# Attention decode with an MLP: output weights loaded later, a part of them by 32 one-row GpSimd transfers that alternate with 2-byte ones

## The chip, the cores and the metric

The kernel runs on one core of one Trainium2 chip. The metric is the time of the core for one execution in microseconds (us), measured on the device. Every figure of a kernel below is the median of its runs unless it says otherwise.

In the profile, PE is the tensor engine, DVE the vector engine, ACT the scalar engine, POOL the GpSimd engine and SP the SyncE engine. SP issues nearly all the loads. A load is carried out by the core's 16 DMA engines: the trace has 16 completion records for it, and the 128 packets of a 2048 KB block, 0.614 us each, over 16 engines make the 4.9 us in which such a block lands.

## The reference, cut to what matters

```python
B, Sq, D, Hq, Hkv, W, Dh, F = 8, 1, 448, 16, 8, 1024, 256, 1792
g = sigmoid((x * gate_w).sum(-1))                 # x: [8, 1, 448] bf16
q = x @ wq                                        # wq: [448, 4096]
a = softmax(q @ k[last 1024].T / 16) @ v[last 1024]   # 8 batches x 8 K/V heads
a = a @ wo                                        # wo: [4096, 448]
b = gelu(layernorm(x) @ w1 + b1) @ w2 + b2        # w1: [448, 1792], w2: [1792, 448]
out = g * a + (1 - g) * b
```

There are 77.7 MB to read and very little arithmetic on each byte. Most of the bytes are the 32 key and value blocks of 2048 KB (2 MiB). `w2`, the MLP output weights, has only 1.6 MB.

## The kernel before

All large loads are issued by SP in one order, the *plan*. They go into a ring of nine slots of 16 KB in each of 128 partitions. `pump` issues the next load of the plan when the slot that it reuses has been read; so the plan's item i waits until item i − 9 has been used up.

```python
    RING = 9
    LAG = 2
...
    def pump():
        while len(slots) < min(len(plan), consumed[0] + RING):
            t = ring.tile([P, SLOT], BF16, tag="slot", name="slot")
            plan[len(slots)](t)
            slots.append(t)
...
    w2_v = B_w2.rearrange("(p c) n -> p (c n)", c=NF)    # 128 rows of 6272 elements
...
    add_kv("k", A_k_cache, 0, parts=2)
    add(("wq", 0), rows_loader([wq_m[:, 0 : 2 * HD]]))
    add(("wq", 1), rows_loader([wq_m[:, 2 * HD : 3 * HD], wq_t]))
    add(("w1",), rows_loader([w1_m, w1_t]))
    add(("w2",), rows_loader([w2_v]))                    # fifth in the plan
    for u in range(1, NQ):
        add_kv("k", A_k_cache, u)
        if u >= LAG:
            add_kv("v", A_v_cache, u - LAG)
```

In what follows K3 is the key block of turn 3, V5 the value block of turn 5, and so on. The order of the plan from the fifth item on is w2, K1, K2, V0, K3, V1, K4, V2, K5, V3, K6, V4, K7, V5 and so on, and at the end the output projection weights `wo` in six pieces.

The compute side runs in one order on each engine. For every turn, DVE transposes two halves of a key block, PE makes the scores, ACT the exponentials, and PE multiplies with the value block of two turns earlier. The MLP output stands ahead of the loop:

```python
    hs = mlp_hidden()
    for hf in range(NH):
        scores(0, hf)
    mlp_out(hs)                       # 56 matmuls on w2, then 4 for the bias b2
    for u in range(1, NQ):
        turn_keys(u, 0)
        scores(u, 0)
...
        top(u - 1)
        share(u - 1)
        turn_keys(u, 1)
        if u >= LAG:
            values(u - LAG)
            invert(u - LAG)
        scores(u, 1)
        expo(u - 1)
```

GpSimd fills one tile with zeros (it is free at 5.6 us) and does nothing after that.

Of the kernel before, what the change touches and what calls it, by code (L numbers as in the profile page):

```python
# [11 lines left out]
BF16 = mybir.dt.bfloat16  # L12
# [6 lines left out]
def kernel(  # L19
# [15 lines left out]
    nc = tc.nc  # L35
    P = nc.NUM_PARTITIONS

    NB, Sq, D = A_x.shape
# [13 lines left out]
    NF = F // P  # L52
# [17 lines left out]
    NJ8 = HPQ * NJ  # L70
    WO_PARTS = [[(0, NJ8)]] * (NHQ - 1) + [[(0, 4), (4, 6), (6, 8)]]
    RING = 9
    LAG = 2
    NK = 4
    NPAR = 2
# [5 lines left out]
    xf = A_x.rearrange("b s d -> (b s) d")  # L81
# [3 lines left out]
    consts = ctx.enter_context(tc.tile_pool(name="consts", bufs=1))  # L85
    ring = ctx.enter_context(tc.tile_pool(name="ring", bufs=RING))
    ktpool = ctx.enter_context(tc.tile_pool(name="ktpool", bufs=3))
    epool = ctx.enter_context(tc.tile_pool(name="epool", bufs=2))
    opool = ctx.enter_context(tc.tile_pool(name="opool", bufs=LAG + 1))
    ps_s = ctx.enter_context(tc.tile_pool(name="ps_s", bufs=2, space=PSUM))  # L90
# [8 lines left out]
# [6 lines that stand above are left out]
    def done(n=1):  # L105
        consumed[0] += n
        pump()

    def kv_loader(src, u, parts):
        b, half = divmod(u, Hkv // QUAD)  # L110
        v = src[b, half * QUAD : (half + 1) * QUAD, kv_base:Sk, :].rearrange(
            "a (s c) d -> s a (c d)", c=NCK
        )

        def load(t):
            n = NCK * Dh // parts
            for i in range(parts):
                nc.sync.dma_start(  # L118
                    t[:, i * n : (i + 1) * n], v[:, :, i * n : (i + 1) * n]
                )  # L120

        return load

    def rows_loader(pieces):
        def load(t):
            o = 0
            for ap in pieces:
                n = 1
                for s in ap.shape[1:]:
                    n *= s  # L130
                dst = t[:, o : o + n]
                if len(ap.shape) == 3:
                    dst = dst.rearrange("p (a n) -> p a n", a=ap.shape[1])
                nc.sync.dma_start(dst, ap)  # L134
                o += n

        return load
# [3 lines left out]
    def add(key, loader):  # L141
        index[key] = len(plan)
        plan.append(loader)

    def add_kv(name, src, u, parts=1):
        add((name, u), kv_loader(src, u, parts))
# [5 lines left out]
    w2_v = B_w2.rearrange("(p c) n -> p (c n)", c=NF)  # L152
# [3 lines left out]
    add(("wq", 0), rows_loader([wq_m[:, 0 : 2 * HD]]))  # L156
    add(("wq", 1), rows_loader([wq_m[:, 2 * HD : 3 * HD], wq_t]))
    add(("w1",), rows_loader([w1_m, w1_t]))
    add(("w2",), rows_loader([w2_v]))
    for u in range(1, NQ):  # L160
        add_kv("k", A_k_cache, u)
        if u >= LAG:
            add_kv("v", A_v_cache, u - LAG)
    for u in range(NQ - LAG, NQ):
        add_kv("v", A_v_cache, u)
    for q in range(0, NHQ, 2):
# [11 lines left out]
    def slot(*key):  # L178
        return slots[index[key]]

    x_sb = consts.tile([NB, D], BF16)
    pump()
    nc.scalar.dma_start(x_sb[:], xf)
# [19 lines left out]
    def tiles(ps):  # L203
        return [
            (ps[32 * i : 32 * i + NB, :], slice(i * DO, (i + 1) * DO))
            for i in range(OT)
        ]
# [75 lines left out]
    for kk in range(NK // NJ):  # L283
        for par in range(NPAR):
# [4 lines left out]
                .to_broadcast([P, QUAD, BLK]),  # L289
            )  # L290
    nc.gpsimd.memset(qw[:], 0.0)  # L291

    def norm_and_gate():
        stats = consts.tile([NB, nc.vector.BN_STATS_DIM], F32)
# [57 lines left out]
    def turn_keys(u, hf):  # L352
        kn = slot("k", u)
        kt = ktpool.tile([P, CH, NK, BLK, NPAR], BF16, tag="kt", name="kt")
        KT[u, hf] = kt
        nc.vector.transpose(  # L356
            kt[:].rearrange("p c k x r -> p (c k x r)").bitcast(WORD),
            kn[:, hf * CH * Dh : (hf + 1) * CH * Dh].bitcast(WORD),
        )
        if hf == NH - 1:  # L360
            done()
# [55 lines left out]
    def scores(u, hf):  # L417
        if hf == 0:
            S[u] = ps_s.tile([P, W], F32, tag="S", name="S")
        cols = slice(hf * CH * BLK, (hf + 1) * CH * BLK)  # L420
        kt = KT.pop((u, hf))
        nc.tensor.matmul(  # L422
            S[u][:, cols], lhsT=foreign[:], rhs=place[:], start=True, stop=False
        )
        for k in range(NK):
            for par in range(NPAR):
                j, m = k // (NK // NJ), k % (NK // NJ) * NPAR + par
                nc.tensor.matmul(  # L428
                    S[u][:, cols],
                    lhsT=qw[:, j, u, m * RQ : m * RQ + P],  # L430
                    rhs=kt[:, :, k, :, par],
                    start=False,
                    stop=(k == NK - 1 and par == NPAR - 1),
                )
# [3 lines left out]
    def top(u):  # L438
        mx = epool.tile([P, 1], F32, tag="mx", name="mx")
        nc.vector.reduce_max(mx[:], S[u][:], axis=AXIS.X)  # L440
        m4 = epool.tile([P, QUAD], F32, tag="m4", name="m4")
        nc.vector.tensor_scalar_mul(m4[:], block[:], mx[:])  # L442
        soft[u] = m4
# [23 lines left out]
    def turn(u):  # L467
        E, rowsum = soft.pop(u)
        ET = epool.tile([P, NCK // PAIR, BLK, PAIR], BF16, tag="ET", name="ET")
        nc.vector.transpose(  # L470
            ET[:].rearrange("p c r i -> p (c r i)").bitcast(WORD),
            E[:].rearrange("p c x i -> p (c x i)").bitcast(WORD),
        )
        soft[u] = (ET, rowsum)
# [3 lines left out]
    def total(u):  # L478
        ET, rowsum = soft.pop(u)
        den[u] = ps_sm.tile([P, 1], F32, tag="sm", name="den")  # L480
        nc.tensor.matmul(  # L481
            den[u][:], lhsT=rowden[:], rhs=rowsum[:], start=True, stop=True
        )
        soft[u] = ET
# [3 lines left out]
    def invert(u):  # L488
        rsel[u] = opool.tile([P, RQ], F32, tag="rsel", name="rsel")
        rb = epool.tile([P, 1], F32, tag="rb", name="rb")  # L490
        nc.vector.reciprocal(rb[:], den.pop(u)[:])  # L491
        nc.scalar.activation(rsel[u][:], sel2[:], ACT.Copy, scale=rb[:])  # L492
# [19 lines left out]
    def gather(u):  # L512
        first = soft.pop(u)
        os_ = epool.tile([P, Dh], F32, tag="os", name="os_")
        nc.vector.scalar_tensor_tensor(
            os_[:],
            in0=PO[:, 1, :],
            scalar=own[:, 1:2],
            in1=first[:],
            op0=ALU.mult,  # L520
            op1=ALU.add,
        )
        soft[u] = os_

    def finish(u):
        b, half = divmod(u, Hkv // QUAD)
        os_, rs = soft.pop(u), rsel.pop(u)
        sm = ps_sm.tile([P, NJ, RQ], F32, tag="sm", name="fin")
        for j in range(NJ):
            nc.tensor.matmul(  # L530
                sm[:, j, :], lhsT=os_[:, j::NJ], rhs=rs[:], start=True, stop=True
            )
        nc.scalar.copy(  # L533
            oT[:, half * RQ : (half + 1) * RQ, :, b].rearrange("p h j -> p j h"), sm[:]
        )
# [49 lines left out]
    def mlp_out(hs):  # L585
        bb = ps_misc.tile([P, DO], F32, tag="misc", name="bb")
        nc.vector.memset(bb[:], 0.0)
        for c in range(NF):
            w = slot("w2")
            for dst, cols in tiles(bb):  # L590
                nc.tensor.matmul(
                    dst,
                    lhsT=hs[:, c, :],
                    rhs=w[:, c * D + cols.start : c * D + cols.stop],
                    start=(c == 0),
                    stop=False,
                )
        for dst, cols in tiles(bb):
            nc.tensor.matmul(
                dst, lhsT=ones_r[:], rhs=b2_r[:, cols], start=False, stop=True  # L600
            )
        done()
        nc.scalar.activation(mixb[:], bb[:], ACT.Copy, scale=gg_s[:, 1:2])
# [5 lines left out]
    hs = mlp_hidden()  # L609
    for hf in range(NH):  # L610
        scores(0, hf)
    mlp_out(hs)
    for u in range(1, NQ):
        turn_keys(u, 0)
        scores(u, 0)
        if u >= LAG + 1:
            gather(u - LAG - 1)
        if u >= LAG:
            turn(u - LAG)
            total(u - LAG)  # L620
        if u >= LAG + 1:
            finish(u - LAG - 1)
# [3 lines that stand above are left out]
        if u >= LAG:  # L626
            values(u - LAG)
            invert(u - LAG)
        scores(u, 1)
        expo(u - 1)  # L630
    u = NQ - 1
# [98 lines left out]
```

## Time and profile before

| what | value | where it is read |
|---|---|---|
| time | 192.22 us (192.21 to 192.5, 3 runs) | the runs |
| DMA rate | 409 to 441 GB/s, nearly everywhere | row GB/s |
| one 2048 KB block | lands every 4.89 us | landings in the trace |
| one 16,384 B packet on one engine | 0.614 us | packets in the trace |
| compute in one turn of 9.78 us | DVE about 7.1 us, PE about 6.9 us | groups of instructions |

The first view is from the page of the kernel before: the span, the busy tenths of PE, DVE and DMA in 40 equal slices of 4.8 us with the GB/s of each slice, the SP queue with its packets, megabytes and share of the 16 engines' time, and the chain of waits that ended last.

```profile
span 190.2 us, 2502 instructions
...
PE   0037799896848775796669874848396839687572
...
DVE  7866256798949494949494949495868677685300
...
DMA  5999999999999999999999999999999999999990
GB/s 194 413 424 428 426 431 433 427 420 427 427 434 420 431 417 441 424 424 434 424 431 429 424 420 438 424 427 424 427 434 434 420 420 431 431 431 420 409 373 26
...
q1 hardware_dynamic: 6512, 77.67, 96.7%
...
DMA 77%; PE 12%; DVE 7%; SPq 1%; ACT 1%; issue 1%
```

DMA stands at 9 (90% or more) in every slice but the first and the last, at about 425 GB/s, and the chain that ended last is DMA for 77% of the span. PE and DVE have gaps everywhere. So the loads bound the kernel, and anything that lets the DMA engines stand idle, or makes one of them end later, is paid for in full (in the result below the last load lands 20.6 us later and the time is 20.5 us longer).

Two groups of instructions of the same page (busy time, mean ns of one, then the idle time before them and what ended it) say what compute waits for.

```profile
L356 DVE STREAM_TRANSPOSE kt<-slot 128x2048 int32<-128x2048 int32 x32 | 73.7, 2306 | 34.4 <-DMA slot<-in_A_k_cache_dram 34.4
L428 PE MATMUL S<-kt,qw 128*128 128x512 bf16 x256 | 70.2, 421 | 34.5 <-DVE kt L356 30.1
```

DVE waits 34.4 us for key blocks to land, and PE waits for DVE. This is the slack of about 2.7 us in a turn that can be used to catch up after a stall.

The last view of before is one window, 36 to 47 us. This is where the changed kernel loads `w2`; here it holds plain key and value blocks.

```profile
core 0: us, PE busy (x) PEld busy (x) DVE busy (x) ACT busy (x) POOL busy (x), PEclk, DMA share, GB/s
36.00:47.00 11.00, 9.52 (x56) 4.28 (x55) 10.03 (x10) 3.56 (x6) 0.00 (x0) 1.00 1.01 427
```

The last figure is the rate: 427 GB/s.

### The profile page before, as it was taken

The numbers are of one execution on the slowest core, as the hardware profiler recorded it, in microseconds if no ns is written. First come the engines' busy times: TensorE is split into PE (matmuls) and PEld (weight loads), VectorE is DVE, ScalarE is ACT, GpSimd is POOL, SyncE is SP. The second block draws the span as 40 slices with busy tenths as digits, with TensorE's granted clock in tenths as the row PEclk, the third lists the DMA queues.
The fourth block names the chain that finished last, engine by engine and source line by source line (L and its number), as shares of the span: only waits on it lengthen the run. The fifth ranks groups of instructions, "written<-read, shape, count | busy, mean of one in ns | idle before, by whom it ended". The sixth has DMA issues, their size and how long they took to land.

```text
span 190.2 us, 2502 instructions
## 1 busy us (share of the span) xinstructions
PE 128.5 (68%) x1013; PEld 67.1 (35%) x1022; DVE 128.0 (67%) x186; ACT 43.1 (23%) x91; POOL 5.0 (3%) x7
## 2 busy tenths in 40 slices
PE   0037799896848775796669874848396839687572
PEld 0021783442413342344234433324142414244261
DVE  7866256798949494949494949495868677685300
ACT  2030230034030404040403140404022400335200
POOL 8100000000000000000000000000000000000000
PEclk9999999999996999699975999999799987999555
DMA  5999999999999999999999999999999999999990
GB/s 194 413 424 428 426 431 433 427 420 427 427 434 420 431 417 441 424 424 434 424 431 429 424 420 438 424 427 424 427 434 434 420 420 431 431 431 420 409 373 26
DMA packets 6734, 77.85 MB, mean 409 GB/s; under 512 B 945, under 2 KB 1346, under 8 KB 1986
## 3 DMA queue, kind: packets, MB, share of 16 engines
q1 hardware_dynamic: 6512, 77.67, 96.7%
q8 instruction: 8, 0.13, 0.3%
q10 hardware_dynamic: 210, 0.02, 0.1%
q14 instruction: 4, 0.03, 0.0%
HBM read 77.68 MB, written 0.01 MB: 409 GB/s over the span
## 4 chain that ended last, share of the span: by engine, by line
DMA 77%; PE 12%; DVE 7%; SPq 1%; ACT 1%; issue 1%
DMA slot<-in_A_k_cache_dram 40%; DMA slot<-in_A_v_cache_dram 20%; DMA slot<-in_A_wo_dram 10%; DMA slot<-in_A_wq_dram 7%; PE S L428 6%; DVE kt L356 5%; PE hT L553 2%; PE hT L543 1%; DVE mx L440 1%; SPq L118 1%; SPq L134 1%; PE Sq L370 1%; PE qt L385 1%; ACT qs L380 1%; PE qp L398 1%
## 5 line engine op out<-in xcount | busy, mean ns | idle before, releaser
L356 DVE STREAM_TRANSPOSE kt<-slot 128x2048 int32<-128x2048 int32 x32 | 73.7, 2306 | 34.4 <-DMA slot<-in_A_k_cache_dram 34.4
L428 PE MATMUL S<-kt,qw 128*128 128x512 bf16 x256 | 70.2, 421 | 34.5 <-DVE kt L356 30.1
L428 PEld LDWEIGHTS <-qw 128*128 128x128 bf16 x256 | 26.5, 104 | 71.9 <-issue 51.1
L457 ACT ACTIVATE E<-S,nmx 128x1024 bf16<-128x1024 f32 x16 | 22.2, 1387 | 2.5 <-DVE nmx L454 2.5
L533 ACT CAST oT<-fin 128x16 bf16<-128x16 f32 x16 | 3.6, 226 | 78.7 <-PE fin L530 78.7
L440 DVE TENSOR_REDUCE mx<-S 128x1 f32<-128x1024 f32 x16 | 19.0, 1187 | 1.2 <-PE S L428 1.2
L500 PE MATMUL PO<-slot,ET 128*16 128x512 bf16 x256 | 18.3, 410 | 1.4 <-DMA slot<-in_A_v_cache_dram 1.4
L509 ACT ACTIVATE first<-PO,own 128x256 f32<-128x256 f32 x16 | 7.6, 473 | 28.2 <-PE PO L500 28.2
L470 DVE STREAM_TRANSPOSE ET<-E 128x512 int32<-128x512 int32 x16 | 11.2, 698 | 2.2 <-ACT E L457 2.2
L422 PE MATMUL S<-place,foreign 128*128 128x512 bf16 x23 | 9.2, 400 | 0.1
L448 PE MATMUL mz<-m,same 128*128 128x4 f32 x32 | 6.2, 265 | 4.1 <-ACT oT L533 4.1
L481 PEld LDWEIGHTS den<-rowsum,rowden 128*128 128x128 f32 x32 | 6.7, 214 | 3.3 <-issue 1.0
L500 PEld LDWEIGHTS <-ET 128*16 128x16 bf16 x256 | 5.3, 91 | 6.0 <-issue 2.3
L448 PEld LDWEIGHTS mz<-m,same 128*128 128x128 f32 x32 | 5.0, 195 | 6.0 <-ACT oT L533 5.3
L422 PEld LDWEIGHTS <-foreign 128*128 128x128 bf16 x32 | 3.2, 100 | 8.5 <-issue 6.7
L481 PE MATMUL den<-rowsum,rowden 128*128 128x1 f32 x32 | 5.0, 226 | 0.4 <-ACT E L457 0.4
L370 PE MATMUL Sq<-slot,xT 128*8 128x512 bf16 x32 | 3.9, 615 | 1.9 <-DMA slot<-in_A_wq_dram 1.9
L413 DVE CAST qw<-qp 32x512 bf16<-32x512 f32 x4 | 2.8, 688 | 3.4 <-ACT qw L411 3.4
L492 ACT ACTIVATE rsel<-sel,rb 128x8 f32<-128x8 f32 x16 | 4.7, 297 | 1.1 <-DVE rb L491 1.1
L671 PE MATMUL A_ps<-slot,oP 128*8 128x112 bf16 x128 | 4.0, 290 | 1.2 <-DMA slot<-in_A_wo_dram 1.2
L291 POOL MEMSET qw<- 128x5120 bf16 x1 | 4.4, 4364 | 0.0
L442 DVE TENSOR_SCALAR m<-block,mx 128x4 f32<-128x4 f32 x16 | 3.7, 230 | 0.6
(135 smaller groups left out, 81.7 us busy)
## 6 DMA issues: line engine op xcount, KB each, us to landing
slot<-in_A_v_cache_dram SPq DMA_DIRECT2D x16, 2048.0 KB, 36.2
slot<-in_A_k_cache_dram SPq DMA_DIRECT2D x15, 2048.0 KB, 39.1
slot<-in_A_wo_dram SPq DMA_DIRECT2D x3, 896.0 KB, 31.0
slot<-in_A_k_cache_dram SPq DMA_DIRECT2D x2, 1024.0 KB, 7.4
slot<-in_A_wq_dram SPq DMA_DIRECT2D x1, 2048.0 KB, 11.7
slot<-in_B_w_dram SPq DMA_DIRECT2D x1, 1568.0 KB
slot<-in_B_w_dram SPq DMA_DIRECT2D x1, 1344.0 KB
slot<-in_A_wq_dram SPq DMA_DIRECT2D x1, 1024.0 KB, 13.5
```

What stands on the lines that cost most here:

```text
L356: nc.vector.transpose(kt[:].rearrange("p c k x r -> p (c k x r)").bitcast(WORD), kn[:, hf * CH * Dh : (hf + 1) * CH * Dh].bitcast(WORD),)
L370: nc.tensor.matmul(Sq[32 * t : 32 * t + NB, n * QN : (n + 1) * QN], lhsT=xT[:, r + half, :], rhs=w[:, o + c : o + c + QN], start=(r == 0), ...
L422: nc.tensor.matmul(S[u][:, cols], lhsT=foreign[:], rhs=place[:], start=True, stop=False)
L428: nc.tensor.matmul(S[u][:, cols], lhsT=qw[:, j, u, m * RQ : m * RQ + P], rhs=kt[:, :, k, :, par], start=False, stop=(k == NK - 1 and par = ...
L440: nc.vector.reduce_max(mx[:], S[u][:], axis=AXIS.X)
L448: nc.tensor.matmul(mz[:], lhsT=same[:], rhs=m4[:], start=True, stop=True)
L457: nc.scalar.activation(E[:].rearrange("p c x i -> p c i x"), S.pop(u)[:].rearrange("p (c i x) -> p c i x", i=PAIR, x=BLK), ACT.Exp, bias=n ...
L470: nc.vector.transpose(ET[:].rearrange("p c r i -> p (c r i)").bitcast(WORD), E[:].rearrange("p c x i -> p (c x i)").bitcast(WORD),)
L481: nc.tensor.matmul(den[u][:], lhsT=rowden[:], rhs=rowsum[:], start=True, stop=True)
L492: nc.scalar.activation(rsel[u][:], sel2[:], ACT.Copy, scale=rb[:])
L500: nc.tensor.matmul(PO[32 * t : 32 * t + PAIR * RQ], lhsT=ET[:, c, 0:RQ, :], rhs=vn[:, PAIR * c * Dh : PAIR * (c + 1) * Dh], start=(c < QUA ...
L509: nc.scalar.activation(first[:], PO[:, 0, :], ACT.Copy, scale=own[:, 0:1])
```

## The change

The intent was to take `w2` out of the early part of the plan, so that key and value blocks come earlier, and to give a part of it to the idle GpSimd queue. `w2` moves to eighth place, behind V0. SP loads its rows 0 to 95, and the last 1411 elements of rows 96 to 127. The first 4861 elements (9722 B) of those 32 rows go by one GpSimd transfer for each row. 4861 is a prime number. After each of them comes a GpSimd transfer of one 2-byte element into a scratch tile that nobody reads. The MLP output matmuls move into turn 2, behind the first `values`.

```diff
--- before.py
+++ after.py
@@ -70,6 +70,8 @@
     NJ8 = HPQ * NJ
     WO_PARTS = [[(0, NJ8)]] * (NHQ - 1) + [[(0, 4), (4, 6), (6, 8)]]
     RING = 9
+    NE = 32
+    NPRIME = 4861
     LAG = 2
     NK = 4
     NPAR = 2
@@ -156,11 +158,17 @@
     add(("wq", 0), rows_loader([wq_m[:, 0 : 2 * HD]]))
     add(("wq", 1), rows_loader([wq_m[:, 2 * HD : 3 * HD], wq_t]))
     add(("w1",), rows_loader([w1_m, w1_t]))
-    add(("w2",), rows_loader([w2_v]))
+
+    def w2_load(t):
+        nc.sync.dma_start(t[0 : P - NE, 0 : NF * D], w2_v[0 : P - NE])
+        nc.sync.dma_start(t[P - NE : P, NPRIME : NF * D], w2_v[P - NE : P, NPRIME:])
+
     for u in range(1, NQ):
         add_kv("k", A_k_cache, u)
         if u >= LAG:
             add_kv("v", A_v_cache, u - LAG)
+        if u == LAG:
+            add(("w2",), w2_load)
     for u in range(NQ - LAG, NQ):
         add_kv("v", A_v_cache, u)
     for q in range(0, NHQ, 2):
@@ -178,6 +186,7 @@
     def slot(*key):
         return slots[index[key]]
 
+    step = consts.tile([1, NE * 8], BF16)
     x_sb = consts.tile([NB, D], BF16)
     pump()
     nc.scalar.dma_start(x_sb[:], xf)
@@ -289,6 +298,14 @@
                 .to_broadcast([P, QUAD, BLK]),
             )
     nc.gpsimd.memset(qw[:], 0.0)
+    w2_t = slot("w2")
+    for i in range(NE):
+        spans = [
+            (w2_t[P - NE + i : P - NE + i + 1, 0:NPRIME], w2_v[P - NE + i : P - NE + i + 1, 0:NPRIME]),
+            (step[:, i * 8 : i * 8 + 1], xf[0:1, 0:1]),
+        ]
+        for dst, ap in spans[::1]:
+            nc.gpsimd.dma_start(dst, ap)
 
     def norm_and_gate():
         stats = consts.tile([NB, nc.vector.BN_STATS_DIM], F32)
@@ -609,7 +626,6 @@
     hs = mlp_hidden()
     for hf in range(NH):
         scores(0, hf)
-    mlp_out(hs)
     for u in range(1, NQ):
         turn_keys(u, 0)
         scores(u, 0)
@@ -626,6 +642,8 @@
         if u >= LAG:
             values(u - LAG)
             invert(u - LAG)
+        if u == LAG:
+            mlp_out(hs)
         scores(u, 1)
         expo(u - 1)
     u = NQ - 1
```

## The prediction

> **What bounds it now.** The DMA engines. The rows by slice show them 90% or more busy at 409 to 438 GB/s from the second slice to the thirty-eighth; the chain of waits that ended last is 77% DMA. A 2048 KB key or value block lands every 4.89 us; one 16,384 B packet takes 0.614 us (27 GB/s per engine). Compute hides behind it: one turn of the loop has 9.78 us of loads, but about 7.1 us of DVE work (two key transposes of 2.3, a maximum of 1.19, a turn of 0.7, small ones) and about 6.9 of PE work.
>
> **What changes.** No byte is saved. (a) The MLP output weights move from fifth in the load plan to eighth; their 1.2 us of matmuls move behind the first values, at about 43.6 us in the timeline. In a full queue this order is worth nothing at the end. (b) The first 9,722 B of 32 rows go to GpSimd, each followed by a 2-byte transfer: 64 issues, eight outstanding. SyncE issues one more (0.54 us, hidden).
>
> **Costs.**
> 1. Engines. [...] The slowest engine ends the loads, and the last landings already spread over 1.8 us: +0.3 to +0.7 us.
> 2. Completion writes: [...] Those of before took 9 ns: 64 of them, an estimated 0.6 us per engine.
> 3. The wait. PE meets the MLP output matmuls in order at about 44 us and stands until the last long transfer has landed. GpSimd is free at 5.6 us. I assume about 1.0 us per issue; the trace has no GpSimd transfer (SyncE issues took 0.54 us, small ScalarE ones 0.28). Then the last lands near 6 + 64 + 4 = 74 us: PE stands some 30 us. The ring still lets eight blocks after the first values load, to about 79.7 us; DMA starves only if the wait ends after about 77. Afterwards compute recovers about 2.6 us per turn, some 30 us in twelve turns; at the end it has about 2 us of slack. So the wait is hidden up to about 1.05 us per issue; each 0.1 us more costs about 6.4 us. This is the steep, uncertain term.
>
> **Prediction.** 193.5 us, range 192.2 to 206; faster by over 2%: 2%, within 2%: 66%, slower by over 2%: 32%.
>
> **What would show it.** PE idle before the first MLP output matmul, ended by a DMA, for tens of us; 64 GpSimd issues ending about 70 us; 420 to 435 GB/s in all slices (hidden), or a dip near slices 16 to 20 (starved); landings of a block's 16 engines spread wider by about 0.7 us afterwards; DVE then not waiting for key blocks until it has caught up.
>
> **What would make it wrong.** GpSimd issues well over 1.05 us each, or completions over 8 us behind 16 KB packets: a loss of 10 us or more. A faster issue (0.7 us) makes the stall short and the result about +1 us. [...] If the slow engines are those that now get less, the time could fall by a few tenths.

The sum of this forecast was 192.2 us of the kernel before, 0.3 to 0.7 for step 1 and 0.6 for step 2, with the wait of step 3 hidden: 193.1 to 193.5 us. The range up to 206 leaves room for a longer wait. In step 3 the 1.0 us per issue and the 4 us after the last issue are the author's assumption; the trace of before did not show them.

## The result, and the profile after

| | before | after |
|---|---|---|
| median | 192.26 us | 212.72 us |
| lowest to highest | 192.21 to 192.5 (4 runs) | 212.63 to 212.88 (4 runs) |
| after / before | | 1.1062 [1.1043 to 1.1082] |

The result is correct and 10.6% slower. Ratios here and below are the mean time of one kernel's fast runs over that of the other's of the same rounds, so not quite the ratio of the medians; the brackets are 95% intervals. Executions over 1.5% slower than the fastest of the same kernel are left out of the means. A difference in us that is worked out from ratios below is their difference times 192.3 us.

The same rows of the page, now of the kernel after; POOL (GpSimd), PEclk (the clock granted to PE, in tenths) and the GpSimd queue q0 are added. A slice is 5.3 us; slices are counted from 0.

```profile
span 210.7 us, 2575 instructions
...
PE   0044799641000000299999888898949675899662
...
DVE  7872257691040000059999999999876849495410
...
POOL 8836444333433320000000000000000000000000
PEclk9999999998555555589999999999988997579755
DMA  6999999999999998076999999999999999999920
GB/s 203 433 397 426 411 408 377 222 324 407 397 414 421 416 424 337 33 292 236 429 426 417 448 407 435 437 414 442 429 417 438 414 435 432 420 432 412 407 103 10
...
q1 hardware_dynamic: 6528, 77.36, 90.0%
q0 software_dynamic: 2048, 0.32, 1.0%
...
DMA 63%; DVE 28%; POOL 4%; PE 2%; issue 1%; POOLq 0%
```

Five things are to be seen here.

1. PE stands in slices 10 to 15 and DVE in 12 to 16: a wait of tens of us. PEclk is 5 in slices 10 to 16, while PE has nothing to do, and 8 or 9 again from slice 17 to 32, where compute catches up. The clock is not the cause.
2. GB/s falls to 222 and 324 in slices 7 and 8, while DMA stays at 9. The engines are busy, but move little.
3. DMA falls to 0 and GB/s to 33 in slice 16, and stays low to slice 18. Here the engines are empty.
4. The last two slices have 103 and 10 GB/s while DVE has almost nothing left to do. DMA shows 2 and 0 there, as a mean over 16 engines.
5. GpSimd's queue q0 has 2048 packets for 64 transfers, 32 for each. It moved only 0.32 MB and took 1.0% of the engines' time.

The groups of the kernel after, in the form of the earlier ones; L308 is the line with the GpSimd transfers.

```profile
L373 DVE STREAM_TRANSPOSE kt<-slot 128x2048 int32<-128x2048 int32 x32 | 73.6, 2301 | 24.4 <-DMA slot<-in_A_k_cache_dram 24.4
L445 PE MATMUL S<-kt,qw 128*128 128x512 bf16 x256 | 67.2, 407 | 14.8 <-DVE kt L373 10.6
...
L608 PE MATMUL bb<-slot,hs 128*8 128x112 bf16 x56 | 1.5, 294 | 38.1 <-DMA slot<-in_B_w_dram 38.1
...
L308 POOL DMA_DIRECT2D slot<-in_B_w_dram x32 | 16.7, 522 | 26.6 <-DMA slot<-in_B_w_dram 26.4
...
L308 POOL DMA_DIRECT2D step<-in_A_x_dram x32 | 16.6, 518 | 14.2 <-DMA step<-in_A_x_dram 13.9
```

The MLP output matmuls waited 38.1 us for a DMA. An issue on GpSimd takes 0.52 us of that engine, but GpSimd waited 26.6 and 14.2 us in addition, for earlier transfers to land: it keeps eight outstanding (the ninth is issued at 11.51 us, after the first has landed at 11.23). DVE's wait for key blocks is 24.4 us now instead of 34.4: it used up slack to catch up.

Timeline of the kernel after (start, length, engine, line, what, in brackets the wait before it):

```profile
88.16 1.48 PE L608 MATMUL bb<-slot,hs 128*8 128x112 bf16 x56 [38.09 <-DMA slot<-in_B_w_dram]
...
89.68 0.54 SPq L120 DMA_DIRECT2D slot<-in_A_k_cache_dram  x1
...
97.06 0.54 SPq L120 DMA_DIRECT2D slot<-in_A_v_cache_dram  x1
```

The wait ends at 88.16 us. Only then can SP issue K7, whose slot is that of `w2`, and V5 after it, whose slot is that of K3. Two windows of the kernel after (36 to 47 us, where it loads `w2`, and 80 to 92 us):

```profile
core 0: us, PE busy (x) PEld busy (x) DVE busy (x) ACT busy (x) POOL busy (x), PEclk, DMA share, GB/s
36.00:47.00 11.00, 6.90 (x34) 3.42 (x33) 9.19 (x9) 1.44 (x2) 3.63 (x7) 1.00 1.00 269
80.00:92.00 12.00, 3.50 (x66) 2.18 (x68) 0.40 (x1) 1.69 (x3) 0.00 (x0) 0.52 0.41 161
```

In the first window the rate is 269 GB/s instead of 427 at a full DMA share (1.00). In the second the share is 0.41.

How long the 2-byte transfers of the kernel after took from issue to landing:

```profile
DMA to landing us min/median/max: 5.8/9.8/11.9
```

Eight outstanding, each 9.8 us to landing, make one every 9.8 / 8 = 1.22 us.

The trace also has the completion record of each DMA engine for each load. From them comes the following table of our own (issue, then the landing of the engine in the middle, the fifteenth and the last of the 16, in us):

```
before                 issue   median  15th    last
K1                      9.47    29.37   30.00   30.81
V4                     44.48    78.44   79.72   79.74
K7                     45.53    83.33   84.62   84.63
V5                     52.41    88.23   89.50   89.52
last piece of wo      167.97   186.32  186.49  186.51

after                  issue   median  15th    last
K1                      9.16    31.19   32.66   41.46
V4                     54.66    84.15   85.78  100.50
K7                     89.68    96.78   97.47  105.38
V5                     97.06   104.27  104.69  110.27
last piece of wo      188.61   201.49  202.92  207.07
```

From K1 on one engine of 16 is late: 9 us behind the fifteenth at K1, 15 us at V4, and still 4 us at the end. I call its distance from the median the *lag*: 16.4 us at V4, 8.6 at K7, 6.0 at V5, 5.6 at the end (0.2 at the end of before). The last landing moved by 207.07 − 186.51 = 20.6 us, which is the whole loss of about 20.5 us.

So there were four suspects: the wait of PE and what it starves, the one late engine, the low rate around 42 us, and the work of the GpSimd transfers themselves.

### The profile page after: what moved, and what is told of

Read it like the earlier page. It is cut to its first block, busy times and chain, and to the rows that moved or that the text cites. A ratio compares the mean times of both kernels' runs of the same rounds, so it can differ in the third digit from the quotient of the medians.

```text
span 210.7 us, 2575 instructions
## 1 busy us (share of the span) xinstructions
PE 126.0 (60%) x1014; PEld 66.8 (32%) x1022; DVE 127.5 (61%) x186; ACT 43.1 (20%) x91; POOL 38.1 (18%) x71
## 3 DMA queue, kind: packets, MB, share of 16 engines
q0 software_dynamic: 2048, 0.32, 1.0%
## 4 chain that ended last, share of the span: by engine, by line
DMA 63%; DVE 28%; POOL 4%; PE 2%; issue 1%; POOLq 0%
DMA slot<-in_B_w_dram 37%; DVE kt L373 18%; DMA slot<-in_A_v_cache_dram 17%; DMA slot<-in_A_wo_dram 9%; DVE mx L457 5%; DVE ET L487 2%; POOL qw L300 2%; PE S L445 1%; DVE m L459 1%; POOL slot L308 1%; POOL step L308 1%; PE bb L608 1%; DVE nmx L471 0%; DVE rb L508 0%; PE A_ps L689 0%
## 5 line engine op out<-in xcount | busy, mean ns | idle before, releaser
L373 DVE STREAM_TRANSPOSE kt<-slot 128x2048 int32<-128x2048 int32 x32 | 73.6, 2301 | 24.4 <-DMA slot<-in_A_k_cache_dram 24.4
L445 PE MATMUL S<-kt,qw 128*128 128x512 bf16 x256 | 67.2, 407 | 14.8 <-DVE kt L373 10.6
L445 PEld LDWEIGHTS <-qw 128*128 128x128 bf16 x256 | 26.0, 102 | 50.3 <-issue 27.4
L608 PE MATMUL bb<-slot,hs 128*8 128x112 bf16 x56 | 1.5, 294 | 38.1 <-DMA slot<-in_B_w_dram 38.1
L308 POOL DMA_DIRECT2D slot<-in_B_w_dram x32 | 16.7, 522 | 26.6 <-DMA slot<-in_B_w_dram 26.4
L308 POOL DMA_DIRECT2D step<-in_A_x_dram x32 | 16.6, 518 | 14.2 <-DMA step<-in_A_x_dram 13.9
L608 PEld LDWEIGHTS <-hs 128*8 128x8 bf16 x56 | 1.2, 122 | 38.6 <-issue 38.6
```

Of the source, the lines that this page charges most:

```text
L308: nc.gpsimd.dma_start(dst, ap)
L373: nc.vector.transpose(kt[:].rearrange("p c k x r -> p (c k x r)").bitcast(WORD), kn[:, hf * CH * Dh : (hf + 1) * CH * Dh].bitcast(WORD),)
L445: nc.tensor.matmul(S[u][:, cols], lhsT=qw[:, j, u, m * RQ : m * RQ + P], rhs=kt[:, :, k, :, par], start=False, stop=(k == NK - 1 and par = ...
L608: nc.tensor.matmul(dst, lhsT=hs[:, c, :], rhs=w[:, c * D + cols.start : c * D + cols.stop], start=(c == 0), stop=False,)
```

## The experiments

Twelve kernels were run. All gave correct results. Short diffs are against the kernel after. The theories that the expectations speak of are these. COUNT: the number of GpSimd transfers sets when PE's wait ends, and that sets the time. Its rival, PILE-UP, was that the loss comes from the bytes of the long rows on one engine (FIRST ENGINE: one row falls on the same engine every time, two rows on the same two). TURNS: a GpSimd transfer waits for turns behind the large packets of the other queue. SPLIT: cutting `w2` by rows makes it slow.

### e1: the long ones alone

```diff
-        for dst, ap in spans[::1]:
+        for dst, ap in spans[:1]:
```

> The 32 two-byte GpSimd transfers are taken out; the 32 long ones stay. In the changed kernel (212.7 us) 64 GpSimd transfers completed at one per about 1.23 us, the PE waited for them until 88.2 us, and one of the 16 engines landed every block 9 to 14 us after the others. Theory COUNT (each transfer costs the same turn behind the big packets, whatever it carries): 32 of them end near 6 + 32 x 1.23 + 3 = 48 us, the PE wait shrinks from 38 us to some 5 us, DMA is not starved. Theory PILE-UP (it is the bytes on one engine): [...]the long ones now spread two to each engine, and the 16 landings of a block are within 2.5 us of each other again; time 192.5 to 195 us. Rival about the pile-up: [...]the slow engine has another cause; then one engine still lags by about 11 us and the time stays at 200 us or more although the PE wait is short.

Measured: 212.41 us (211.73 to 212.91), ratio 1.1045 [1.1018 to 1.1072]. The rows by slice of this kernel, and its MLP output matmuls in the timeline:

```profile
PE   0023268937637949684966698484999596669773
...
DMA  5999999999999999999999999999999999992000
GB/s 214 422 392 421 408 398 388 230 335 405 434 402 425 421 440 434 415 431 421 437 425 425 434 420 431 421 437 428 421 431 425 434 428 425 411 394 108 25 29 12
```

```profile
60.71 1.48 PE L608 MATMUL bb<-slot,hs 128*8 128x112 bf16 x56 [2.87 <-DMA slot<-in_B_w_dram]
```

The wait ended at 60.7 us instead of 88.2, and PE waited only 2.9 us for it. No slice shows empty engines before the end. COUNT was right that the wait nearly goes, though not on the end near 48 us: the last of the 32 landed at 53.7, and what PE then still waited for was SP's own part of `w2`, which the late engine landed at about 60.6 to 60.8. But the time did not improve: the rival held on the time. The end of the GB/s row, 108 25 29 12, is one engine at its own rate of about 27 GB/s (16,384 B in 0.614 us) for some 15 us. The records agree: the last `wo` piece landed at 190.46 (median), 191.89 (15th) and 206.29 us (last). K1 had been at 31.37, 33.06 and 50.97. The 2-byte transfers did not decide where the long ones went: with or without them, one engine got the load (at K1 it was 10.3 us behind the median in the kernel after, 19.6 us here).

### e2: a length that can be divided

```diff
-    NPRIME = 4861
+    NPRIME = 4864
```

4864 can be divided by 16 (16 × 304), 4861 cannot.

> The long GpSimd transfers get 4864 elements instead of 4861[...]; still 64 transfers. COUNT: they still complete at one per about 1.23 us, the PE still waits until 80 to 88 us, DMA still starves for several us; time 200 to 208 us. PILE-UP as the only cause: no engine takes all the bytes, the last engine of a block lands within 2.5 us of the first, the waits of GpSimd shorten and the time falls to 192.5 to 196 us. If both matter: no lagging engine (about 4 to 5 us less at the end), wait until about 83 us, 203 to 206 us.

Measured: 200.99 us (200.06 to 202.95), ratio 1.0467 [1.0405 to 1.0529]. No engine lags any more: V4 landed at 84.45 (median) and 85.79 (last). PE waited until 80.1 us, 8 us less than in the kernel after, so the late engine had also held up the transfers that PE waits for. K7 and V5 landed 5.15 and 6.41 us after the block before each, 0.3 and 1.5 us more than the 4.89 us of a full queue. So some 9 us of loss is left with no late engine and about 1.8 us of starvation. Something else cost about 7 us.

### e3 and e4: the later place alone, with and without 64 tiny transfers

```diff
# e4: w2 whole, in the late place; no GpSimd transfer at all
-        nc.sync.dma_start(t[0 : P - NE, 0 : NF * D], w2_v[0 : P - NE])
-        nc.sync.dma_start(t[P - NE : P, NPRIME : NF * D], w2_v[P - NE : P, NPRIME:])
+        nc.sync.dma_start(t[:, 0 : NF * D], w2_v)
-    w2_t = slot("w2")      # and the loop with the GpSimd transfers
# e3: the same, and 64 transfers of 2 bytes that nobody waits for
+    for i in range(2 * NE):
+        nc.gpsimd.dma_start(step[:, i * 4 : i * 4 + 1], xf[0:1, 0:1])
```

> All MLP output weights by SyncE again (in their late place), and GpSimd issues 64 two-byte transfers that nobody on PE waits for. COUNT: these also complete at one per about 1.2 us and end near 80 us, although they carry nothing; as nothing waits for them the time is that of the order alone plus at most 1 to 2 us: 192 to 194 us. PILE-UP as the cause of the slow completion: tiny ones complete at the rate of their issue, 0.52 us each, and end near 42 us.

> Only the place of the MLP output weights and of their matmuls is changed, no GpSimd transfer. Prediction as on record: worth nothing, 191.7 to 192.7 us. If the place itself costs (a rival for part of the 20 us), more than 194 us.

Measured: e4 192.41 us, ratio 1.0012 [0.9993 to 1.003]; e3 193.01 us, ratio 1.0041 [1.0025 to 1.0056]. The later place is worth nothing and costs nothing. 64 GpSimd transfers with all their completion packets cost (1.0041 − 1.0012) × 192.3 = 0.6 us; the two intervals overlap a little, so this is small but not sharply measured. From issue to landing in e3, then its GpSimd row and GB/s:

```profile
DMA to landing us min/median/max: 4.9/8.2/10.3
```

```profile
POOL 8938644454444400000000000000000000000000
...
GB/s 212 394 402 429 431 418 426 415 427 421 424 424 419 421 428 435 424 421 431 431 428 429 428 417 431 431 428 431 424 421 434 431 428 428 424 424 423 413 342 11
```

The tiny ones took 8.2 us each and the last landed at about 76 us, although nothing in this kernel slows the loads (the GB/s row is flat). So even a GpSimd transfer of 2 bytes is slow to complete behind a full queue, 8.2 us here and 9.8 in the kernel after, and the work that 64 of them give the engines is small, 0.6 us.

### e5: the row cut alone

```diff
-        nc.sync.dma_start(t[P - NE : P, NPRIME : NF * D], w2_v[P - NE : P, NPRIME:])
+        nc.sync.dma_start(t[P - NE : P, 0 : NF * D], w2_v[P - NE : P])
```

The GpSimd transfers are gone too. SP loads rows 0 to 95 and then rows 96 to 127, each with all its columns.

> No GpSimd transfer; SyncE loads the MLP output weights in two pieces, rows 0 to 95 and rows 96 to 127, in their late place. Theory SPLIT: the piece of 96 rows itself runs at about half rate (its 12,544 B packets took 0.89 to 0.92 us in the runs with the cut, 0.474 whole), and this is the 5 to 6 us by which the engines that do not lag were late in three runs: 195 to 198 us, and about 260 to 330 GB/s between 36 and 44 us. Rival: the GpSimd transfers beside it slow that stretch; then this is 192.0 to 193.0 us, as the order alone (192.41).

Measured: 198.3 us (197.63 to 199.02), ratio 1.0321 [1.0286 to 1.0357], slightly more than SPLIT expected. The window of e5:

```profile
core 0: us, PE busy (x) PEld busy (x) DVE busy (x) ACT busy (x) POOL busy (x), PEclk, DMA share, GB/s
36.00:47.00 11.00, 6.32 (x78) 3.41 (x80) 8.10 (x10) 2.22 (x4) 0.00 (x0) 0.94 0.99 264
```

264 GB/s at a DMA share of 0.99, as in the kernel after (269). The packets of 12,544 B took 0.877 us (median) instead of 0.473 in e4. Two pieces with the same bytes as one cost (1.0321 − 1.0012) × 192.3 = 5.9 us against e4.

### e6 and e8: two rows in each transfer, and all 32 in one

```diff
-    for i in range(NE):    # the loop with the GpSimd transfers
# e6
+    for i in range(0, NE, 2):
+        nc.gpsimd.dma_start(
+            w2_t[P - NE + i : P - NE + i + 2, 0:NPRIME],
+            w2_v[P - NE + i : P - NE + i + 2, 0:NPRIME],
+        )
# e8
+    nc.gpsimd.dma_start(w2_t[P - NE : P, 0:NPRIME], w2_v[P - NE : P, 0:NPRIME])
```

No 2-byte transfers in either. The row cut of the kernel after is kept.

> 16 GpSimd transfers of two rows of 4861 instead of 32 of one, no two-byte ones. Theory FIRST ENGINE: [...]one row always falls on the same engine and two rows on the same two; two of the 16 landings of a block lag by 6 to 8 us, the other 14 are together; time 202 to 206 us. Rival CURSOR: two engines in turn; all engines get the same, the landings stay within 2.5 us and the time is 196 to 198 us. Rival PRIME: an undividable row length puts all on one engine whatever the rows; one engine lags by 12 to 15 us, 211 to 213 us.

> One GpSimd transfer of 32 rows of 4861 for the same bytes. [...]there is no lagging engine and no wait for it: what is left is the cut itself. SPLIT: the same as the run with the cut alone within 1 us (195 to 198 us). Rival: 192 to 193 us if neither costs anything.

Measured: e6 207.11 us, ratio 1.078 [1.0761 to 1.0798], a little over the expected range; e8 199.34 us (198.31, 199.24 and 199.45 in three fast runs, and 201.3 in a slow one that is left out of the ratio), ratio 1.035 [1.032 to 1.0381], about 1 us over e5 and over the expected range. The GB/s row of e6, then of e8:

```profile
GB/s 218 420 379 373 327 384 427 273 282 418 384 414 436 427 430 427 423 433 427 427 433 420 431 420 430 433 430 420 423 433 430 430 427 423 428 410 405 121 41 10
```

```profile
GB/s 188 419 328 425 425 427 428 339 248 397 427 430 430 433 423 427 427 430 427 427 423 430 425 427 427 430 423 427 427 433 430 430 420 427 427 433 416 414 266 3
```

In e6 two engines lag: K1 landed at 34.29 (14th), 44.56 (15th) and 45.87 us (last). The end of its row, 121 41 10, is that of two engines. In e8 none lags: the last `wo` piece landed at 190.48, 191.59 and 192.11 us. So FIRST ENGINE holds as far as landings can show it, since the records do not name the engine: with one row in a transfer one engine lags (e1, 15.8 us behind the median at the end), with two rows two do (e6, 7.2 and 10.5 us). Both rivals of e6 fall: the landings did not stay within 2.5 us, and it was not one engine. The price, with the same bytes and the same cut, is (1.1045 − 1.035) × 192.3 = 13.4 us for one engine (e1 against e8) and 8.3 us for two (e6 against e8).

### e7: packets of half the size

```diff
-        add_kv("k", A_k_cache, u)
+        add_kv("k", A_k_cache, u, parts=2)
```

The same for the value blocks; everything else as in e3.

> As the run with 64 two-byte GpSimd transfers that nobody waits for (they took about 1.0 to 1.24 us each once key and value packets of 16,384 B flowed), but every key and value block is loaded in two halves, so that packets are 8192 B and take 0.31 us. Theory TURNS: a transfer needs two turns on each engine, each behind one big packet; with half packets a transfer needs about 0.62 us, and the 64 end near 46 to 55 us instead of 76. Rival: a fixed latency of about 8 to 10 us per transfer with eight outstanding; then they end near 76 us again. The time of the whole kernel is not the question (192 to 196).

Measured: 195.68 us in only two runs (195.32 and 196.03), ratio 1.0178 [1.0151 to 1.0204]. Its time from issue to landing and its GpSimd row:

```profile
DMA to landing us min/median/max: 4.8/5.6/7.3
```

```profile
POOL 8937848778500000000000000000000000000000
```

The tiny ones took 5.6 us instead of 8.2 and ended at 57.8 instead of about 76 us, a little later than expected. In the steady stretch the median interval from one completion to the next was 0.63 us instead of 1.23 (over all 64, some of which came sooner, the mean is 0.82 instead of 1.10). A packet of 8192 B took 0.312 us in e7, one of 16,384 B 0.613 in e3 (medians). Both rates are two turns behind a packet: 2 × 0.312 = 0.62 and 2 × 0.613 = 1.23 us. TURNS held in both rates. It agrees with 32 packets for each transfer, on average 2 on each of the 16 engines, though nearly all have only 4 bytes (1984 of the 2048 in the kernel after). That e7 is about 2.6 us slower than e3 is not explained; two runs are few, and halving the packets changes more than this.

### e9 and e10: cut by columns

```diff
# e9: two SP pieces with all 128 rows, no GpSimd transfer
+        nc.sync.dma_start(t[:, 0:NPRIME], w2_v[:, 0:NPRIME])
+        nc.sync.dma_start(t[:, NPRIME : NF * D], w2_v[:, NPRIME:])
# e10: as many bytes for GpSimd as after, but as 128 rows of 1216 elements in one transfer
+        nc.sync.dma_start(t[:, 1216 : NF * D], w2_v[:, 1216:])
...
+    nc.gpsimd.dma_start(w2_t[:, 0:1216], w2_v[:, 0:1216])
```

> The control for the cut: SyncE loads the MLP output weights in two pieces again, but cut by columns (4861 and 1411), each over all 128 rows; no GpSimd transfer. If it is the cut by rows that costs 6 us (96 and 32 of the 128 rows), this is 192.0 to 193.0 us and GB/s stays over 410 between 36 and 47 us. Rival: a second piece as such, or a short one, costs; then 195 us or more.

> The aim of the change without its three costs: one GpSimd transfer of the same bytes (0.31 MB), as the first 1216 columns of all 128 rows, and SyncE the other columns of all rows. Theory: no cut by rows, no pile-up, no late completion: 192.0 to 193.2 us. It should not beat the kernel before, since DMA moves the same bytes. If the GpSimd path itself costs, more than 194.

Measured: e9 193.21 us, ratio 1.0047 [1.0032 to 1.0062], 0.2 us over the expected range; e10 192.51 us, ratio 1.0009 [0.9992 to 1.0026]. The window of e9:

```profile
core 0: us, PE busy (x) PEld busy (x) DVE busy (x) ACT busy (x) POOL busy (x), PEclk, DMA share, GB/s
36.00:47.00 11.00, 8.74 (x107) 4.34 (x107) 8.62 (x11) 3.91 (x7) 0.00 (x0) 1.00 1.01 428
```

428 GB/s, where the cut by rows had 264. So it is not two pieces that are slow, but pieces of few partitions. And e10 gives GpSimd practically the same number of bytes as the change did (155,648 elements instead of 155,552), and loses nothing. It is the best form of the change, and it equals the kernel before; no version here beats it.

### e11 and e12: the wait alone

`w2` is whole and loaded by SP in the late place, so there is no cut and no long row. The bias `b2` is loaded by 64 GpSimd transfers of 7 elements, and the bias matmuls wait for it. e12 puts 10 tiny transfers ahead of them.

```diff
-    nc.scalar.dma_start(b2_r[:], B_b2.rearrange("(o d) -> o d", o=1))
+    for i in range(10):                       # 0 in e11
+        nc.gpsimd.dma_start(step[:, i * 4 : i * 4 + 1], xf[0:1, 0:1])
+    for i in range(64):
+        nc.gpsimd.dma_start(b2_r[:, i * 7 : i * 7 + 7], b2_f[:, i * 7 : i * 7 + 7])
```

> The wait alone: all weights whole by SyncE in their late place, but the output bias (896 B) comes by 64 GpSimd transfers of 7 elements, and the bias matmuls at the end of the MLP output wait for the last. They should land near 77 us, so that PE stands for some 33 us. If such a wait is hidden up to about 77 us, as the prediction computed, the time is 192.4 to 195 us. Rival: PE standing that long costs by itself: over 200 us.

> The same with ten two-byte GpSimd transfers ahead, so that the wait ends near 88 us, as in the changed kernel. Past the 77 to 79.7 us at which the last allowed block has landed, DMA runs dry, and the loss should be about as long as the overrun plus the 2.6 us gap of the next block: 9 to 14 us, 201 to 206 us. Rival (the wait costs nothing, all of the loss is cut and pile-up): under 195 us.

Measured: e11 196.16 us, ratio 1.0208 [1.0193 to 1.0224]; e12 207.14 us, ratio 1.0778 [1.0753 to 1.0804]. Both are above what was expected. The slices of e11, then of e12:

```profile
DMA  5999999999999999959999999999999999999980
GB/s 200 440 385 390 358 420 419 418 430 417 420 427 422 427 424 430 430 232 427 424 430 430 430 427 429 427 427 427 427 430 424 430 424 427 427 430 420 413 347 11
```

```profile
PE   0046999650000000089998989898989867988662
...
DMA  5999999999999999401999999999999999999980
GB/s 210 425 400 434 401 395 408 421 417 434 421 416 431 421 418 431 179 0 38 399 418 434 430 427 430 422 440 418 427 430 418 446 411 437 424 418 450 399 352 26
```

PE's wait ended at 77.4 us in e11 and at 87.9 us in e12. In e11 one slice falls to 232 GB/s; in e12 one falls to 0 and its neighbours to 179 and 38. The timeline of e12:

```profile
87.93 0.25 PE L611 MATMUL bb<-b_r,ones_r 1*8 1x112 bf16 x1 [17.25 <-DMA b_r<-in_B_b_dram]
...
95.90 0.54 SPq L120 DMA_DIRECT2D slot<-in_A_v_cache_dram  x1
```

One thing differs from the kernel after: here the matmuls on `w2` ran before the wait, so K7 could be issued before it too (at 48.0 us in e12, 48.6 in e11). V5 was issued 8.0 us after the wait's end (95.90 − 87.93), and 8.0 us in e11 too (85.39 − 77.42). It needs the slot of K3, and K3's two transposes and scores stand behind PE's and DVE's backlog. It then landed 103.11 − 84.25 = 18.9 us after K7, 14.0 us more than the 4.89 of a full queue; in e11 2.4 us more. So 10.5 us more of wait cost 11.6 us of starvation: beyond the threshold all is paid. (The whole losses against e4 are 3.8 and 14.7 us; the rest has the 0.6 us of the 64 transfers in it.) The threshold follows from e11: to leave no gap, V5 would have had to be issued 2.4 us earlier, so the wait may last until about 75 us. In e11 the loads were already about 2 us late by then (V4 landed at 80.40 us in the median, 78.44 before; why is not shown), so for loads on time it is about 73 us by estimate.

## Why the prediction was wrong, point by point

In short: step 1, the placement, failed in its mechanism. Its error also went into step 3, the wait, whose mechanism was right and whose length was mis-sized. And the row cut was not priced at all.

**What bounds the kernel: right.** DMA stayed the limit, and each part of the loss is a way in which DMA engines moved less: slowed, empty, or one alone at work.

**The later place is worth nothing: right.** e4 is at 1.0012.

**Step 2, completion writes, 0.6 us in each engine: right in size, in part by luck.** e3 against e4 is 0.6 us. But the prediction counted one packet of 9 ns on each engine for a transfer, and the queue had two (2048 packets in e3), which is 64 × 2 × 9 ns = 1.2 us. The measured difference is too small against its noise to tell the two apart.

**Step 3, the wait: the mechanism was right, the term was mis-sized.** The prediction says "I assume about 1.0 us per issue" and "the last lands near 6 + 64 + 4 = 74 us". GpSimd's own issue took 0.52 us; the assumption should have been about completion. The last of the 64 landed at 89.15 us, so they took (89.15 − 5.6) / 64 = 1.31 us each, and the last *long* one landed at 87.92 us and released PE, 14 us later than predicted. Most of these 14 us are not the rate of the transfers. In e3, with neither cut nor long rows, the 64 end at 75.8 us, or 1.10 us each, hardly later than predicted. In e2, with the cut and with 4864 elements in a row, where no engine lags, PE is released at 80.1 us. The other 8 us are the late engine's: fifteen of the 16 completions of the last long transfer were in by 83.41 us, 4.5 us before the last, and earlier ones that came late had held up later issues, as only eight are outstanding. So the two errors meet here: step 1 is the larger part of what step 3 got wrong. The prediction had the price of this ("each 0.1 us more costs about 6.4") and put the threshold at 1.05 us. What it lacked was the reason of the rate, which e3 and e7 show: two turns behind a packet of 0.613 us give 1.23 us in the steady stretch. With a second packet counted on every engine, it could have been estimated from the 0.614 us that the prediction itself quotes. The threshold was also too high: the prediction has "about 77", e11 says 75, or about 73 for loads on time. The prediction counted the blocks that the ring lets load; what came last was V5, which waited another 8.0 us behind the backlog of compute. "What would make it wrong" did name completions "over 8 us behind 16 KB packets" and a loss of 10 us or more; they took 9.8 us.

**Step 1, the placement: wrong.** The forecast took the long rows to be spread over eight engines, at +0.3 to +0.7 us. What the runs show is the load of all 32 rows on one engine (after, e1), and on two when a transfer has two rows (e6). In the kernel after each of these rows was one packet of 9722 B (32 such packets, 0.371 us each in the median). Why the rows come to one engine, and which it is, is not shown. What the load costs can be summed from the packets: in e1 the 32 packets of 9722 B took 0.437 us each in the mean, 14.0 us in all on the one engine. The measured lag at the end of e1 was 15.8 us (206.29 − 190.46), and e8, with the same cut and no late engine, still has a lag of 1.6 us (192.11 − 190.48); so little is left to explain there. In e6 the same sum is 16 × 0.412 = 6.6 us on each of two engines, against lags of 7.2 and 10.5 us at the end; there a part stays open.

**Not priced: the cut by rows.** The prediction wrote only "SyncE issues one more (0.54 us, hidden)". The cut alone costs 5.9 us (e5), and a cut by columns 0.7 us (e9 against e4). In e5 the piece of 32 rows, 401 KB, took 1.85 us from the median landing of the piece before it to its own, or 217 GB/s. The piece of 96 rows, 1.20 MB, took 5.3 us, or 227 GB/s, not three quarters of the 427 of a full load. Why few rows are slow is open: no run shows which engine writes which rows.

**How the parts make 20.6 us.** One at a time they come to more: 5.9 for the cut (e5), 13.4 for the late engine (e1 against e8), and (1.0778 − 1.0012) × 192.3 = 14.7 for a wait to 88 us (e12), together 34. In the changed kernel they hide each other. The landings of before and after, worked out from the two tables above (shift of the median landing, lag of the last engine):

```
                    shift of the median    lag, before    lag, after
V4                  + 5.7 us               1.3            16.4
K7                  +13.5                  1.3             8.6
V5                  +16.0                  1.3             6.0
last piece of wo    +15.2                  0.2             5.6
```

Up to V4 the median is 5.7 us late: the cut, and GpSimd's share of turns. After V4 fifteen engines have nothing to do until K7 and V5 can be issued, at 89.68 and 97.06 us. K7's and V5's intervals are 12.63 and 7.49 us instead of 4.89, so 7.7 + 2.6 = 10.3 us of starvation. V5 lands at 104.27 in the end, and in e12, where no cut came first, it lands at 103.11 after nearly the same end of the wait (87.93 against 88.16). So the wait alone sets that landing, and the 5.7 us of the cut are inside it. While the fifteen stand idle, the late engine catches up: its lag falls from 16.4 to 6.0. What is left is 15.2 us of the median and 5.4 of lag, 20.6 in all. Most of the starvation is the late engine's doing too, as it had delayed the end of the wait: without it (e2) the wait ended at 80.1 us and 1.8 us were starved, and the whole loss was 11.4 us smaller, (1.1062 − 1.0467) × 192.3. This also says why taking away the wait alone (e1) gains nothing: the late engine then never catches up, and keeps 15.8 us to the end.

**Compute recovers about 2.6 us in a turn: right.** After the wait the turns ran at 6.9 us instead of 9.78 (from a key transpose on DVE to that of the next turn, 94.33, 101.22, 108.12), which recovers 2.9 us in each. Once V5 was issued, compute had no more part in the loss: from then on the blocks land 4.9 us apart again.

**Left open.** Which engine it is that lags, as the trace has no names for the completions, and why the rows come to it. Why pieces of 32 or 96 rows are slow. Why the lag in e1 was larger for a time, 19.6 us at K1 (50.97 − 31.37). The part of the lag in e6. The 2.6 us of e7. The 2 us by which the loads of e11 were late before its wait ended.

## What to carry to other kernels

A transfer on a second queue behind a queue full of large packets completes at a rate set by those packets (here two turns, so 1.23 us each at 16 KB), not by its issue time; count the transfers that somebody waits for and multiply. Give every load all 128 partitions and cut it by columns: here rows sent one at a time loaded one engine (13.4 us, e1 against e8), a quarter of the rows got 217 GB/s instead of 427, while the same bytes as one [128 x 1216] transfer cost nothing (e10, ratio 1.0009). And when several faults are in one change, look at the landing of every engine for a few blocks, since taking one fault away may only uncover the next.
